# PSUM banks begun by ScalarE or VectorE with a summand, seven products for four more tiles, and three inverses on GpSimd, in a linear-attention block with a feed-forward part

## The chip, the cores and the metric

The kernel runs on one core of one Trainium2 chip. The metric is device time in microseconds of one execution; lower is better. The engines are named as in the profile: PE (TensorE products), PEld (its weight loads), DVE (VectorE), ACT (ScalarE), POOL (GpSimd) and SP (SyncE, which here only issues DMA). PSUM, where PE writes its products, has eight banks of 512 columns of 32 bits for each of the 128 partitions. All eight are one tile here, `banks`.

## What is computed

One transformer block over 2048 tokens of width 640, in bfloat16, with 32 heads of 20. First a linear attention with softmax features (Hedgehog), then a feed-forward part of width 1728, each behind a layer norm and with a residual:

```python
n   = layernorm(x)
q, k, v = n @ wqkv                        # 32 heads of 20
pq, pk  = q @ w_phi, k @ w_phi            # per head
phi_q = [softmax(pq), softmax(-pq)]       # 40 features; phi_k likewise
kv, z = phi_k^T v, sum over tokens of phi_k
o   = (phi_q @ kv) / (phi_q . z + 1e-6)
h   = x + o @ wo
out = h + silu(layernorm(h) @ w1) @ w2
```

## The kernel before

The tokens are cut into 16 tiles of 128. Everything of one tile is cut into named steps, such as `K3` (the keys of tile 3). The list `ORDER`, written out in full, gives the steps in the one order in which they are recorded; no scheduler moves them. Each step puts its instructions into the queues of its engines, and every queue runs in that order. So the order of steps decides what stands ahead of what on each engine, and semaphores between the engines do the rest.

The steps that the text names, with t the tile:

- `st`, `xn`: moments and normalised rows of x (L509, L528). `K`, `V`, `Q`: products with the key, value and query weights (L605, L643). `ex`, `su`, `rk`, `sc`: exponentials of the keys on ACT, their sums on DVE (L664), the inverses on ACT and the scaling on DVE (L677). `kv`: the sum over tokens phi_k^T v on PE (L696). `bd0`, `bd1`: DVE copies that sum out as a block-diagonal matrix after `kv15` (L705).
- `qe`: exponentials of the queries on ACT (L767). `qs`: their sums on DVE (L771). For tiles 0 to 5 `ql` takes the inverse as Ln and Exp on ACT (L782), `qi` the ratio of the two sums on POOL (L791) and `qr` the scaling on DVE (L802). For tiles 6 to 15 `qr` holds all three on DVE (L785, L791, L802). `qt`: a DMA transpose of the features.
- `D`: features times the block-diagonal matrix on PE (L851). `E`: inverse and division on DVE (L860, L861). `ot`: a DMA transpose. `G` with 0 or 1 for the half of the columns: products with wo on PE (L883), into a pair of banks. `ga`: DVE adds that pair to X, which from then on holds h (L890). `lm`, `ls`: sums and squares of h on ACT (L538, L543). `lr`: the inverse deviation on POOL in three small instructions, the middle one a power (L550, L553, L554). `hn`: the normalised rows on ACT (L560). `ht`: a DMA transpose.
- The feed-forward part goes by units: tiles 0 and 1, 2 to 5, 6 to 9, 10 to 13, 14 and 15. `u` and `s`: the plain way, products with w1 and the silu on ACT, one bank at a time (L966, L989); `u.L` (L977), `s.L` and `lt` are the last 64 columns. Units 6, 10 and 14 take another way for most of the columns: two by two blocks of weights and rows by seven products in place of eight (a Strassen form). It needs sums of weight blocks, `vw` (L1010, made once), and of row blocks, `vt` (L1020). Each group of two banks X and Y is filled by `vA` to `vE` on PE (L1047). Between them ACT saves intermediate states of bank Y into the tile `vr`: `vc1` both halves (L1059), `vc2` and `vc3` one (L1062). `va1` and `va0` add them to the banks on DVE (L1066), and `vs1`, `vs0` are the silus on ACT, from `vr` (L1072). So such a group is A, vc1, B, vc2, C, vc3, D, va1 in a chain between PE and ACT.
- The products with w2 take the seven-product form for every pair of tiles. `T` and `S` are sums of weights and of rows on DVE (L1120, L1137). `p1` to `p7` are the products on PE (L1155), 7 of 320 columns each. `p1`, `p5` and `p6` add up in bank a. `r1`, `r2`, `r3` and `r7` keep an intermediate state of a bank plus X in SBUF, on DVE (L1163). So `p6` waits for `r1`, which must have read bank a, and `p7` waits for `S3`. `w11`, `w12`, `w21` and `w22` add bank and kept state to the output tile on DVE (L1170). `out` stores it.

PSUM banks are handed out by `ps_half` and `ps_two` from a ring, the longest handed out first.

Of the kernel before, what the change touches and what calls it, by code (L numbers as in the profile page):

```python
# [36 lines left out]
qs9 lm2 u0.6 T1.2 s0.0 s0.L ga3 E4 qt6 u0.2 qr8 ls2 T2.2 qt7 s0.6 G50 u0.4 D6 lm3 T3.0 ls3 u0.12 qr9
T4.2 G51 s0.2 u0.10 E6 s0.4 s0.12 ot4 ga5 T3.2 T1.0 S3.0 lt0 u0.8 D7 E7 lr3 lr2 hn3 s0.10 hn2 qt8 G41
G40 p7.0 s0.8 T2.0 p2.0 D8 ot6 lm5 p1.0 ga4 T1.1 T4.0 S1.0 ht2 T2.1 ht3 ls5 lm4 padL1 S2.0 r1.0 G61 ls4
T4.1 r7.0 G60 S4.0 w11.0 p6.0 r2.0 ot7 lr5 E8 hn5 p4.0 lr4 w21.0 ga6 ht5 hn4 p5.0 ht4 p3.0 r3.0 G71 qs11  # L40
lm6 w22.0 qs10 ot8 qt9 G70 u2.L u2.10 w12.0 qr10 qt10 u2.5 ga7 u2.2 u2.9 qr11 u2.6 s2.5 s2.L s2.2 u2.11
s2.10 D9 qt11 s2.6 s2.9 qs12 out1 u2.0 qs13 lm7 out0 G81 E9 s2.11 qr12 D10 ot9 s2.0 G80 ga8 u2.4 D11
qt12 s2.4 ls7 E10 u2.1 u2.8 u2.3 qr13 ls6 qs15 G90 lm8 E11 G91 qs14 lr7 u2.12 ga9 ls8 s2.8 s2.3 lr8 lr6
# [33 lines left out]
def kernel(  # L77
# [65 lines left out]
    def ps_half():  # L143
        ring.append(ring.pop(0))
        return banks[:, ring[-1]]
# [1127 lines left out]
```

## Time and profile before

| | us |
|---|---|
| median of 2 runs (222.33 to 222.44) | 222.38 |
| the profiled execution, its own time | 222.19 |
| its span in the profile | 220.2 |
| PE busy | 215.3 |
| DVE busy | 196.5 |
| ACT busy | 166.1 |
| POOL busy | 71.8 |

The span runs from the first instruction to the end of the last; the execution's own time is about 2 us longer. The granted clock of TensorE is full throughout. A group's mean length of one instruction runs from its start to its end; the next one can start before that, so steps from start to start are shorter than the length. In the windows and in the chain, the first number is microseconds from the start of the span.

### The profile page before, as it was taken

To read this page: it belongs to the slowest core of one execution; us is meant where nothing else is said; L and a number is where in the kernel's file an instruction comes from. 1 tells how busy PE (TensorE), PEld (TensorE's weight loads), DVE (VectorE), ACT (ScalarE), POOL (GpSimd) and SP (SyncE) were. 2 spreads that over 40 slices of the span, in tenths; PEclk is the share of its full clock that TensorE was granted. 3 is DMA by queue.
4 is the path that set the end of the run, shared out by engine and by line. 5 is a ranking of instruction groups with operands and counts; after the bars stand their busy time and mean duration, and the time that the engine had idled before them with its cause. 6 is when DMAs were issued, how large, how long until landed. Compare 5 with 4: busy or idle time off the path is not lost.

```text
span 220.2 us, 5436 instructions
## 1 busy us (share of the span) xinstructions
PE 215.3 (98%) x2076; PEld 163.7 (74%) x2076; DVE 196.5 (89%) x352; ACT 166.1 (75%) x372; POOL 71.8 (33%) x136
## 2 busy tenths in 40 slices
PE   6999999999999999999999999999999999999994
PEld 4877777777777777887746577787888788887773
DVE  3999999999999999999999999999859955887984
ACT  6999899999879899997345986599879966474200
POOL 8399999979300140045000511340002200000000
PEclk9999999999999999999999999999999999999999
DMA  6999839947999786874586876553700124010202
GB/s 165 343 296 131 116 70 266 171 115 129 302 233 177 128 168 92 161 112 89 118 105 155 187 115 127 67 125 68 108 1 4 29 54 63 30 63 12 92 30 89
DMA packets 68159, 27.00 MB, mean 123 GB/s; under 512 B 61159, under 2 KB 67111, under 8 KB 68007
## 3 DMA queue, kind: packets, MB, share of 16 engines
q1 hardware_dynamic: 67335, 26.61, 58.7%
q8 instruction: 16, 0.26, 0.5%
q10 hardware_dynamic: 800, 0.06, 0.3%
q14 instruction: 8, 0.07, 0.1%
HBM read 9.55 MB, written 2.62 MB: 55 GB/s over the span
## 4 chain that ended last, share of the span: by engine, by line
PE 86%; DVE 10%; POOL 2%; issue 1%; ACT 0%; POOLq 0%
PE banks L1155 24%; PE banks L1047 13%; PE banks L605 11%; PE banks L966 11%; PE banks L883 10%; PE banks L643 9%; DVE st L509 4%; PE banks L851 3%; DVE Sk L664 2%; PE banks L696 2%; DVE xn L528 1%; PE banks L977 1%; DVE EK L677 1%; DVE mv L510 1%; DVE WTk L352 0%
## 5 line engine op out<-in xcount | busy, mean ns | idle before, releaser
L605 PEld LDWEIGHTS <-XnT 128*128 128x128 bf16 x300 | 28.4, 98 | 9.4
L528 POOL TENSOR_SCALAR xn<-X,mv,rs 128x640 bf16<-128x640 bf16 x12 | 31.5, 2626 | 0.6 <-ACT rs L518 0.4
L550 POOL TENSOR_SCALAR rs<-mv 128x1 f32<-128x1 f32 x16 | 3.8, 235 | 74.9 <-ACT xn L543 74.6
L1155 PEld LDWEIGHTS <-S 128*128 128x128 bf16 x224 | 21.5, 98 | 7.5
L1155 PE MATMUL banks<-T,S 128*128 128x320 bf16 x168 | 26.7, 299 | 0.0
L966 PE MATMUL banks<-HnT,w_sb 128*128 128x512 bf16 (+1 forms) x145 | 25.8, 328 | 0.0
L1066 DVE TENSOR_TENSOR vr<-banks,vr 128x512 f32<-128x512 f32 x30 | 20.0, 684 | 6.3 <-PE banks L1047 5.4
L883 PE MATMUL banks<-wo_sb,OT 128*128 128x320 bf16 x160 | 25.1, 299 | 0.0
L1072 ACT ACTIVATE shT<-vr 128x512 bf16<-128x512 f32 x30 | 18.1, 626 | 8.4 <-DVE vr L1066 8.3
L1047 PE MATMUL banks<-HnT,w_sb 128*128 128x256 bf16 (+1 forms) x144 | 24.3, 255 | 0.0
L643 PE MATMUL banks<-Wfq,XnT 128*128 128x342 bf16 (+2 forms) x160 | 22.7, 293 | 0.0
L605 PE MATMUL banks<-Wv,XnT 128*128 128x320 bf16 x150 | 22.3, 299 | 0.0
L664 DVE TENSOR_REDUCE Sk<-EK 128x64 f32<-128x1216 bf16 x16 | 21.9, 1391 | 0.2 <-ACT EK L660 0.2
L605 PE MATMUL banks<-Wfk,XnT 128*128 128x304 bf16 x150 | 21.6, 292 | 0.0
L660 ACT ACTIVATE EK<-banks 128x608 bf16<-128x608 f32 x32 | 20.2, 694 | 0.9 <-PE banks L605 0.5
L1155 PEld LDWEIGHTS <-shT 128*128 128x128 bf16 x175 | 16.6, 98 | 5.6
L966 PEld LDWEIGHTS <-w_sb 128*128 128x128 bf16 x145 | 13.8, 97 | 8.3
L883 PEld LDWEIGHTS <-OT 128*128 128x128 bf16 x160 | 15.4, 98 | 5.8
L1163 DVE TENSOR_TENSOR r<-banks,X 128x320 f32<-128x320 f32 x32 | 15.2, 483 | 5.0 <-PE banks L1155 4.9
L643 PEld LDWEIGHTS <-XnT 128*128 128x128 bf16 x160 | 15.0, 97 | 5.4
L989 ACT ACTIVATE shT<-banks 128x512 bf16<-128x512 f32 (+1 forms) x23 | 12.6, 571 | 7.0 <-PE banks L966 7.0
L1155 PE MATMUL banks<-w_sb,shT 128*128 128x320 bf16 (+2 forms) x119 | 17.7, 291 | 0.0
(121 smaller groups left out, 469.2 us busy)
## 6 DMA issues: line engine op xcount, KB each, us to landing
out_dram<-o_t SPq DMA_DIRECT2D x15, 160.0 KB, 1.9
w_sb<-in_B_w_dram SPq DMA_DIRECT2D x5, 432.0 KB, 5.2
w_sb<-in_B_w_dram SPq DMA_DIRECT2D x3, 480.0 KB, 5.2
X<-in_A_x_dram SPq DMA_DIRECT2D x1, 1280.0 KB, 8.5
Wk<-in_A_wqkv_dram SPq DMA_DIRECT2D x5, 160.0 KB, 3.4
Wv<-in_A_wqkv_dram SPq DMA_DIRECT2D x5, 160.0 KB, 6.2
wo_sb<-in_A_wo_dram SPq DMA_DIRECT2D x1, 800.0 KB, 5.0
X<-in_A_x_dram SPq DMA_DIRECT2D x1, 640.0 KB, 6.4
```

Of the source, the lines that this page charges most:

```text
L528: eng.tensor_scalar(out=xn_[t][:], in0=X[:, t, :], scalar1=mv_.pop(t)[:, 0:1], scalar2=rs_.pop(t)[:], op0=ALU.add if t in BY_ROWS else ALU ...
L605: nc.tensor.matmul(ps[:, g, 0:w], XnT[:, c, t * P : (t + 1) * P], W[:, c, g * w : (g + 1) * w], start=(c == 0), stop=(c == C - 1),)
L643: nc.tensor.matmul(ps[:, 0 : e - a], XnT[:, c, t * P : (t + 1) * P], Wfq[:, c, a:e], start=(c == 0), stop=(c == C - 1),)
L660: nc.scalar.activation(E5[:, :, :, b, 0:DR], p4, AF.Exp, scale=sign)
L664: nc.vector.tensor_reduce(sk[t][:], ek[t][:, 0 : H * HF].rearrange("p (q f) -> p q f", f=DH)[:, :, 0:DR], axis=AX.X, op=ALU.add)
L883: nc.tensor.matmul(ps_of["G", t][:, g, 0:HD], ot[t][:, c, :], wo_sb[:, c, g * HD : (g + 1) * HD], start=(c == 0), stop=(c == C - 1),)
L966: nc.tensor.matmul(ps[:, at : at + n], w1_sb[:, c, fc * P : fc * P + P], HnT[u][:, c, 0:n], start=(c == 0), stop=(c == C - 1),)
L1047: nc.tensor.matmul(vb_[u, i, bank][:, at : at + n], left[:, c, f * P : (f + 1) * P], right[:, c, :], start=bool(first) and q == 0 and c == ...
L1066: nc.vector.tensor_tensor(r, two(vb_.pop((u, i, "XY"[j]))), r, op=ALU.add)
L1072: nc.scalar.activation(rows_of(u)[:, f * n : (f + m) * n].rearrange("p (q b n) -> p b q n", q=m, b=2), vr_[u, i][:, 2 - 2 * j : 4 - 2 * j] ...
L1155: nc.tensor.matmul(ps[:, lo:hi], left[:, c, :], right[:, c, lo:hi], start=(c == 0 and k in FIRST), stop=(c == KS - 1 and k in LAST), skip_ ...
L1163: nc.vector.tensor_tensor(r_[t, name][:], ps_of[bank, t][:, 0:HD], X[:, t + i, g * HD : (g + 1) * HD], op=ALU.add)
```

## The change

Five things change together.

1. *Output projection.* `ga` now comes ahead of `G`: ACT copies X into the pair of banks, and the products of `G` add to it without starting the bank anew. `lm` reads h from the banks, writes it to X and takes its sum in the same ACT instruction. DVE has no part in it.
2. *Inner seven products.* `vc1` becomes two copies on ACT: one half of Y goes into bank X, the other to `vr`. `vc3` copies into the other half of X. `vE` adds its products to what stands in X, and `vs0` reads X directly. `va0` goes; `va1` stays. `vr` has two rows in place of four and three buffers in place of two.
3. *Unit of tiles 2 to 5* takes the seven-product form too (`BYSUMS`). So `vw` is wanted earlier, and there is a `vt` for that unit.
4. *Output products.* `r1` and `r3` write their sum (DVE) into the bank of `p2` and `p3`, which add to it. `w11` and `w12` become plain copies on ACT.
5. *Inverses of tiles 13 to 15* become a power on POOL with the ratio behind it on POOL; only the scaling stays on DVE.

A bank is now given back by `release`, after its last reader, and a seeded bank must have been covered by an earlier product. `ORDER` is written anew from the early steps on. The weight loads, the early phase's engines and the sizes of all other products are the same.

```diff
-    def ps_half():
-        ring.append(ring.pop(0))
-        return banks[:, ring[-1]]
+    def ps_half(key, cols=HD, seeded=0, readers=1):
+        k = next(k for k in ring if covered[k] >= seeded)
+        take(key, 0 if seeded else cols, [k], readers)
+        return banks[:, k]
...
     def row_mean(t):
         nc.scalar.activation(
-            xn_[t][:], X[:, t, :], AF.Identity, scale=-1.0 / (D * RD), accum_out=mv_[t][:, 0:1]
+            in_halves(t), ps_of.pop(("G", t))[:, :, 0:HD], AF.Identity, accum_out=mv_[t][:, 0:1]
         )
+        release(("G", t))
...
+    LATE_Q = 13
...
         if t < EARLY_Q:
             nc.scalar.activation(rm[:], ratios(t)[:, :, 1], AF.Ln)
             nc.scalar.activation(rm[:], rm[:], AF.Exp, scale=-1.0)
+        elif t < LATE_Q:
+            nc.vector.reciprocal(rm[:], ratios(t)[:, :, 1])
         else:
-            nc.vector.reciprocal(rm[:], ratios(t)[:, :, 1])
+            nc.gpsimd.tensor_tensor(rm[:], ratios(t)[:, :, 1], minus_t[:].to_broadcast([P, n]), op=ALU.pow)
...
-        eng = nc.gpsimd if t < EARLY_Q else nc.vector
+        eng = nc.vector if EARLY_Q <= t < LATE_Q else nc.gpsimd
...
     def residual(t):
-        xs = X[:, t].rearrange("p (g d) -> p g d", g=2)
-        nc.vector.tensor_tensor(xs, ps_of.pop(("G", t))[:, :, 0:HD], xs, op=ALU.add)
+        ps_of["G", t] = ps_two(("G", t), seeded=HD)
+        act(ps_of["G", t][:, :, 0:HD], in_halves(t))
     def out_projection(t, g):
...
-                start=(c == 0), stop=(c == C - 1),
+                start=False, stop=(c == C - 1), skip_group_check=True,
...
-    BYSUMS = (6, 10, 14)
+    BYSUMS = (2, 6, 10, 14)
...
     def inner_kept(u, i, which):
+        y = two(vb_[u, i, "Y"])
         if which == 1:
-            vr_[u, i] = pools["sums"].tile([P, 4, NU], F32, name="vr", bufs=2)
-            act(vr_[u, i][:, 1:3], two(vb_[u, i, "Y"]))
+            vb_[u, i, "X"] = ps_half((u, i, "X"), seeded=2 * NU)
+            vr_[u, i] = pools["sums"].tile([P, 2, NU], F32, name="vr", bufs=VRB)
+            act(two(vb_[u, i, "X"])[:, 0:1], y[:, 1:2])
+            act(vr_[u, i][:, 1:2], y[:, 0:1])
+        elif which == 2:
+            act(vr_[u, i][:, 0:1], y[:, 1:2])
         else:
-            k = {2: 0, 3: 3}[which]
-            act(vr_[u, i][:, k : k + 1], two(vb_[u, i, "Y"])[:, 1:2])
+            act(two(vb_[u, i, "X"])[:, 1:2], y[:, 1:2])
...
+    def seeded(t, bank, i, g, lo=0, hi=HD):
+        bank += "x" * (lo > 0)
+        ps_of[bank, t] = ps_half((bank, t), seeded=HD)
         nc.vector.tensor_tensor(
-            outs[t + i][:, g * HD + lo : g * HD + hi], ps_of[bank, t][:, lo:hi], r_[t, name][:, lo:hi], op=ALU.add
-        )
+            ps_of[bank, t][:, lo:hi], ps_of["a", t][:, lo:hi], X[:, t + i, g * HD + lo : g * HD + hi], op=ALU.add
+        )
+        release(("a", t))
...
+    def whole(t, bank, i, g, lo=0, hi=HD, eng="ACT"):
+        bank += "x" * (lo > 0)
+        copies[eng](out_of(t + i)[:, g * HD + lo : g * HD + hi], ps_of[bank, t][:, lo:hi])
+        release((bank, t))
```

Three stretches of the order, before and after, that the prediction speaks of. Early keys, before and after:

```
su3 K4 ref5 fq0 rs9 ex4 fq0e rs8 xt6 V4 wq2 ve4 su2 su4 V5 ve5 fq3 K5 rk2 xn7 ref6 xt7 rk3 xn8 fq3e sc2 K6 ex5 sc3 ex6 kv2
su3 K4 ref5 fq0 rs9 ex4 fq0e rs8 xt6 V4 wq2 ve4 V5 fq3 ref6 rk3 ve5 su2 rk2 xn7 xn8 wq4 K5 st15 xn9 K6 xt7 fq3e sc3 sc2 xt8 kv2
```

From the silu of unit 0 to `p6.0`, after:

```
G30 load9 qs11 ga5 s0.6 padL0 s0.L T1.2 s0.2 ls2 G31 G51 qt6 qt7 G50 T1.1 T2.0 T2.2 D6 qs10 ot4 lm5 u0.0 lm3 ls5 s0.10 lt0 qt8
u0.12 vw1.0 u0.4 T3.1 ga4 E6 s0.0 T2.1 T4.2 lr2 D7 s0.4 s0.12 u0.8 ot6 G41 G40 vw1.1 T3.2 qr11 s0.8 ls3 hn2 lm4 vw3.0 S3.0 S1.0
lr5 p1.0 S2.0 r1.0 p7.0 hn5 E7 p6.0 r7.0 ht2 lr3 D8 ls4 r2.0 p2.0 E8
```

From `qs13` to the late scalings, after:

```
qs13 ql13 qi13 vC.2.1 vD.2.0 va1.2.0 vc3.2.1 qt10 G71 ot8 vc1.2.2 vw3.1 vE.2.0 vA.2.3 vB.2.2 vs1.2.0 vs0.2.0 qr12 vD.2.1 G70
vw2.1 vc2.2.2 vC.2.2 vE.2.1 vc1.2.3 lm7 vc3.2.2 vs0.2.1 vB.2.3 vc2.2.3 va1.2.1 vs1.2.1 qs14 ql14 D9 vE.2.2 vC.2.3 vA.2.4 vD.2.2
vA.2.5 vw4.1 vs0.2.2 E9 vc3.2.3 vc1.2.4 ga8 vE.2.3 qt12 vB.2.4 va1.2.2 ot9 out1 vs0.2.3 vD.2.3 vc2.2.4 vs1.2.2 vc1.2.5 G81 vC.2.4
va1.2.3 G80 D10 vc3.2.4 lm8 vB.2.5 vD.2.4 vc2.2.5 out0 vE.2.4 ht6 ga9 qr13 qi14 qr14 vC.2.5 vc3.2.5 E10
```

More of the change, by code (lines that the diff above doesn't have):

```diff
@@ L39 @@
[L39 to L43, printed above, removed]
```

228 lines of the change are left out of this document (121 added, 107 removed).

## The prediction

> **What bounds the kernel now.** I read the page first, then the chain that ended last, then the engines' busy time in a stretch, then single instructions.
>
> ```profile
> span 220.2 us, 5436 instructions
> PE 215.3 (98%) x2076; PEld 163.7 (74%) x2076; DVE 196.5 (89%) x352; ACT 166.1 (75%) x372; POOL 71.8 (33%) x136
> PE 86%; DVE 10%; POOL 2%; issue 1%; ACT 0%; POOLq 0%
> ```
>
> The busy share of PE alone would not prove a bound, but the chain is 86% PE. Its pieces in order of time (start, length, line, count):
>
> ```profile
> 28.94 0.49 PE banks L696 x11
> ...
> 65.16 2.62 PE banks L643 x20
> ...
> 93.75 0.35 PE banks L851 x12
> ...
> 102.44 1.36 PE banks L883 x10
> 103.79 3.80 PE banks L1155 x28
> ...
> 109.54 6.47 PE banks L966 x30
> ...
> 158.27 3.49 PE banks L1047 x32
> ...
> 205.88 11.44 PE banks L1155 x91
> ```
>
> From 28.94 to 217.32 us one PE piece begins where the last ended. So there TensorE never waits, and the time falls only if it gets less work; any wait it meets is added in full. The next question is how much room the other engines have. This is busy time per stretch (columns: span, then PE, PEld, DVE, ACT, POOL with instruction counts, clock, DMA share, GB/s):
>
> ```profile
> 65.12:102.69 37.57, 37.57 (x390) 29.58 (x387) 36.80 (x63) 36.10 (x90) 8.02 (x21) 1.00 0.80 141
> 103.79:141.00 37.21, 37.21 (x310) 23.79 (x308) 36.09 (x65) 21.34 (x44) 7.99 (x20) 1.00 0.67 125
> ```
>
> From bd0 to r1.0 (65 to 103 us) PE, VectorE and ScalarE are all full. Afterwards ScalarE is at 57% and VectorE still at 97%. A change that shifts work from VectorE to ScalarE has room behind 104 us and hardly any ahead of it.
>
> **The change part by part.** *Products of tiles 2 to 5.* Twelve banks of five 512-column products go, six groups of eighteen 256-column products come. L966 runs 30 in 6.47 us, 216 ns each; L1047 runs 32 in 3.49 us, 109 ns each. 60 x 0.216 = 12.94 us against 108 x 0.109 = 11.78 us: **-1.16 us**, all on the path. No other product is added or removed.
>
> *The early order.* In VectorE's queue the second of two key scalings, sc2, releases kv2 on PE. Its neighbours:
>
> ```profile
> 19.77 0.87 DVE L509 BATCH_NORM_STATS2 st<-X 128x6 f32<-128x320 bf16 x2
> ...
> 20.80 1.29 DVE L528 TENSOR_SCALAR xn<-X,mv,rs 128x640 bf16<-128x640 bf16 x1
> ...
> 24.05 4.02 DVE L664 TENSOR_REDUCE Sk<-EK 128x64 f32<-128x1216 bf16 x3
> 27.98 1.55 DVE L677 TENSOR_TENSOR EK<-EK,Rk 128x1280 bf16<-128x1280 bf16 x2
> 29.45 0.88 DVE L509 BATCH_NORM_STATS2 st<-X 128x6 f32<-128x320 bf16 x2
> ```
>
> Before: su3, su2, su4 (1.31 us a step), then sc2 and sc3 (0.735 a step). After: su3, su2, st15 (19.77 to 20.80, 1.03), then sc3 and only then sc2. sc2 starts at 24.05 + 2.62 + 1.03 + 0.735 = 28.44 instead of 27.98, and PE, which does the same work ahead of kv2, waits **+0.45 us** longer.
>
> *VectorE ahead of p6.0.* r1.0 must have read bank a before p6.0 adds to it. The rows for the sums:
>
> ```profile
> 66.80 1.52 DVE L771 TENSOR_REDUCE Sq<-EQa 128x66 f32<-128x1320 bf16 x1
> 68.24 0.35 DVE L860 RECIPROCAL Rd<-banks 128x32 f32<-128x32 f32 x1
> ...
> 95.93 0.81 DVE L890 TENSOR_TENSOR X<-banks,X 128x640 bf16<-128x640 f32 x1
> 96.66 1.05 DVE L1120 TENSOR_TENSOR T<-w_sb 128x960 bf16<-128x960 bf16 x2
> ...
> 98.16 0.35 DVE L860 RECIPROCAL Rd<-banks 128x32 f32<-128x32 f32 x1
> 98.54 0.82 DVE L861 TENSOR_TENSOR O<-banks,Rd 128x640 bf16<-128x640 f32 x1
> 99.28 0.48 DVE L1120 TENSOR_TENSOR T<-w_sb,T 128x640 bf16<-128x640 bf16 x1
> ...
> 102.69 0.48 DVE L1163 TENSOR_TENSOR r<-banks,X 128x320 f32<-128x320 f32 x1
> ```
> ```profile
> L785 DVE RECIPROCAL Rq<-Sq 128x33 f32<-128x33 f32 x10 | 3.5, 354 | 0.0
> L791 DVE TENSOR_TENSOR Rho<-Sq,Rq 128x66 bf16<-128x66 f32 x10 | 2.3, 228 | 0.3
> L802 DVE TENSOR_TENSOR EQb<-EQb,Rho 128x660 bf16<-128x660 bf16 x7 | 3.5, 502 | 0.2
> L1010 DVE TENSOR_TENSOR SW<-w_sb 128x768 bf16<-128x768 bf16 x4 | 2.2, 547 | 0.0
> ```
>
> VectorE needs 37.57 us from bd0 (65.12) to r1.0 (102.69). Six additions ga leave this stretch (0.73 each, 95.93 to 96.66), E7 (98.16 to 99.28, 1.12) and T4.0 (0.48) move behind it: -6.0. But qs10 and qs11 (66.80 to 68.24, 1.44 each), qr11 (0.354 + 0.228 + 0.502 = 1.08) and vw1.0, vw1.1, vw3.0 (0.55 each) move ahead of it, the last three because SW sums are now wanted four tiles earlier: +5.6. Net -0.4, so r1.0 ends 37.2 + 0.48 = 37.7 us after bd0. On PE some blocks that stood ahead of p6.0 now stand behind it: D8 (0.35), G60 with G61 (1.36), p2.0 (a quarter of 3.80, 0.95), together 2.66. From 65.16 to 103.79 PE worked without a gap, 38.63 us; now 35.97. PE would come to p6.0 at 101.1 us and find r1.0 done at 102.8. It waits **+1.8 us**, with 0.1 for the semaphore (1.5 if the moved sums overlap their neighbours by 0.1 each, 2.2 if qr2, whose ql2 now stands behind qe3 on ScalarE, starts late). A wait on a seed ahead of p6.0 (ga2 before G21, ga3 before G30) lies inside this one, since VectorE's queue sets the later end.
>
> *Work moved to ScalarE.* Sixteen additions (L890) become seeds: a ScalarE copy of X into PSUM, ahead of G instead of behind. No ScalarE write into PSUM is in the trace. Rows near it:
>
> ```profile
> L538 ACT ACTIVATE xn<-X 128x640 bf16<-128x640 bf16 x16 | 11.9, 743 | 5.6 <-DVE X L890 4.7 <-DMA HnT<-xn 0.8
> L681 ACT CAST VP<-banks 128x640 bf16<-128x640 f32 x16 | 10.9, 685 | 0.1
> L989 ACT ACTIVATE shT<-banks 128x512 bf16<-128x512 f32 x21 | 12.0, 589 | 7.0 <-PE banks L966 7.0
> L1062 ACT COPY vr<-banks 128x256 f32<-128x256 f32 x30 | 10.8, 371 | 8.3 <-PE banks L1047 8.1
> L1072 ACT ACTIVATE shT<-vr 128x512 bf16<-128x512 f32 x30 | 18.1, 626 | 8.4 <-DVE vr L1066 8.3
> ```
>
> I bound a seed by 0.685 and 0.743 and take 0.72, the middle of the two. lm then reads PSUM instead of X, 0.06 less or the same. The Trainium skill ("ScalarE: Activation LUTs", section "Step-by-step: what each stage is for") holds that ScalarE reaches PSUM faster than SBUF; by it a seed would cost less than 0.685, and no run here shows it. From p6.0 to 141 us, eight seeds add 5.8 us, six groups of tiles 2 to 5 add 6 x (4 x 0.371 + 0.626 + 0.589) = 16.2 for the 12 x 0.589 = 7.1 that go, six last copies w11, w12 add 6 x 0.43 (between L1062 and L989): 21.3 + 5.8 + 9.1 + 2.6 = 38.8 us of durations for a stretch of 37.2 - 1.16 + 1.8 = 37.8. Of some 80 instructions each overlaps the next by about 0.1 us (VectorE's 0.81 long step took 0.73), so about 31 us: full, but possible. I cost it at nothing; the cover is the 16 us that ScalarE had free. VectorE loses fifteen additions va0 and the w11, w12 there; they lay beside PE work and gain nothing.
>
> *Late inverses.* Tiles 13 to 15 take the reciprocal as a power on GpSimd, with the product behind it:
>
> ```profile
> L553 POOL TENSOR_TENSOR rs<-rs,nhalf_t 128x1 f32<-128x1 f32 x16 | 10.9, 681 | 1.3
> L550 POOL TENSOR_SCALAR rs<-mv 128x1 f32<-128x1 f32 x16 | 3.8, 235 | 74.9 <-ACT xn L543 74.6
> L791 POOL TENSOR_TENSOR Rho<-Sq,Rq 128x66 bf16<-128x66 f32 x6 | 2.4, 394 | 17.1 <-ACT Rq L783 17.1
> ```
> ```profile
> OT<-O SPq DMA_TRANSPOSE x16, 2.6
> ```
>
> The last row, of the view of the transfers, is a transpose from issue to landing (2.6 us). A power over one column takes 0.68 us, 0.45 more than the plain L550; over 33 columns none is shown. It costs between 0.7 (columns free, as L791's 66 nearly are) and 0.24 + 33 x 0.45 = 15 us. I take 3 us, the middle in ratio. While it runs, qr14 waits on VectorE with E10 queued behind. E10 cannot begin before D10 has ended, and from qs13's place in the order to there PE has 63 of the 256-column products (6.9), four G halves (2.7) and two D (0.7): 10.3 us, of which qs13 takes 1.44 and 8.9 remain. Two powers and two products, one after the other, and qr14 must fit: 2X + 0.8 + 0.5 <= 8.9, X <= 3.8. Behind it E10 has a lead: G101 comes 6.2 us of products after D10, and E10 with its transpose needs 1.12 + 2.6, so about 2 us more of delay is free and X may be 4.8. At 3 us the cost is nothing.
>
> *Sum against the profiled execution* (222.19 us, 2 us around its span): -1.16 + 0.45 + 1.8 = +1.1, 223.3 us. The shown runs' median, 222.38, is 0.19 above it: **223.5 us**. Against 222.38 that is no change: 2% (4.4 us) is what a measurement of this kernel can tell.
>
> **The rivals.** *A. The products alone decide.* VectorE reaches r1.0 in time because its steps shrink or PE's early wait goes: 222.38 - 1.16 = 221.2, up to 222.4 with a part of the wait. For it: E7 and six ga did leave. Against: the count above has VectorE without a gap in that stretch.
>
> *B. Slower: the power blocks VectorE.* If one power costs X over 4.8 us, each microsecond more is paid twice, since qr14 waits for two. Over 2% slower, 226.8, wants 3.3 us more than the forecast, so it decides from X = 6.5, 0.2 us a column; at X = 8 the time is 230, at 10 it is 234. For it: the one-column row, if each column is paid anew. Against: L791, where 66 columns cost less than one power. The Trainium skill ("GPSIMD Engine Reference", section 3.1 "Elementwise — side-by-side cycle accounting") keeps elementwise work on VectorE, which speaks for B; its 2.6 cycles an element would make 33 columns nearly free, which speaks against it. No trace here settles it.
>
> *C. ScalarE becomes the bound* after p6.0: if its instructions overlap by 0.05 us instead of 0.1 and a tenth is lost to waiting in order (vc1 now stands between A and both B and E), 38.8 - 4 + 3.8 = 38.6 us stand against 37.8, and PE waits 1 to 3 us there: 224.6 to 226.8.
>
> **How the numbers follow.** Forecast (222.4 to 224.6) 0.55, A (221.0 to 222.4) 0.12, C 0.19, B 0.14. The range 221.5 to 227.0 leaves out a part of A and nearly all of B. Faster by over 2% would need 4.4 us from a change that removes 1.16 us of PE work: 0.01, out of A; slower 0.14, from B; the rest is within 2%.
>
> **What would show it.** L1047's successor with 324 + 108 products, PE busy about 1.2 us less in work; kv2 at about 29.4; a PE gap of 1 to 2 us ahead of the first p7.0 and p6.0 with VectorE's S or r as releaser; VectorE without gaps before it. B shows as POOL rows of over 5 us and VectorE waiting on POOL near 125 us; C as PE waits on ScalarE copies between 104 and 140 us. The forecast is wrong if PE shows no gap near 101 us, or gaps behind it that add up to over a microsecond.

## The result, and the profile after

The changed kernel takes 244.52 us (median of 243.48 and 245.57) against 222.38 us: 1.100 times as long, 95% interval 1.079 to 1.120. The forecast was 223.5 us, the range 221.5 to 227.0. So the change is 22 us slower, 10 times what the forecast's own bad terms came to.

First the page of the kernel after: span, busy time, the chain by engine, and the busy tenths of PE with the granted clock, in 40 slices of 6.1 us.

```profile
span 243.5 us, 5588 instructions
PE 221.8 (91%) x2124; PEld 170.8 (70%) x2124; DVE 175.6 (72%) x309; ACT 187.2 (77%) x444; POOL 89.1 (37%) x143
...
PE   7899999999999979579996697299999999999995
...
PEclk9999999999999999959999999779999999999999
...
PE 45%; POOL 15%; DVE 15%; ACT 8%; issue 8%; DMA 6%; SPq 1%; DVEq 0%; ACTq 0%; POOLq 0%
```

Before, PE was busy for 98% of the span and 86% of the chain. Now it is 45% of the chain, and GpSimd, which was 2%, is 15%. The row of PE shows three holes: slices 17 and 18 (97 to 110 us), 22 and 23 (128 to 140) and 25 and 26 (146 to 158). Behind the first and the last the clock row falls too. What PE waited for, from the view of the waits (line, releaser, total, times, longest):

```profile
PE banks L904 <- ACT banks L900: 6.9, 3, 5.7
PE banks L877 <- DVE O L887: 5.9, 2, 3.9
PE banks L1051 <- DVE SW L1014: 1.4, 1, 1.4
PE banks L968 <- DMA HnT<-xn: 1.1, 1, 1.1
```

L900 is the seed `ga`, L877 is `D`, L1014 is `vw`, L968 is `u`. Before, PE had no such wait behind 29 us.

The rest of this document needs a ledger. For each product of the trace I take the time from its start to the next start, less the median of that for its size. The sum of the medians is PE's work: 212.93 us before and 211.79 after, so **-1.14 us**. What is over the median is time lost:

| us lost by PE | 0 to 20 | 20 to 66 | 66 to 95 | 95 to 112 | 112 to 125 | 125 to 145 | 145 to 165 | all |
|---|---|---|---|---|---|---|---|---|
| before | 3.2 | 0.3 | 0 | 0 | 0 | 0 | 0 | 3.3 |
| after | 4.2 | 1.2 | 2.6 | 6.8 | 0.1 | 4.6 | 8.3 | 27.7 |

(For the kernel after the third and fourth columns part at 100 us.) -1.1 of work and +24.4 lost make the 23.3 us between the two spans. Behind 165 us nothing is lost. Three places hold 19.7 of the 24.4.

**The first hole, 100 us.** VectorE's instructions in order of time (start, length, and in brackets the idle time before with its releaser):

```profile
96.27 1.52 DVE L795 TENSOR_REDUCE Sq<-EQb 128x66 f32<-128x1320 bf16 x1
102.63 0.56 DVE L1014 TENSOR_TENSOR SW<-w_sb 128x768 bf16<-128x768 bf16 x1 [4.84 <-DMA EqT<-EQa]
...
103.89 0.82 DVE L887 TENSOR_TENSOR O<-banks,Rd 128x640 bf16<-128x640 f32 x1
```

The 0.56 us sum is `vw1.0`. It waits 4.84 us for a DMA transpose that it has no data from. The tile SW, which it writes, lies in memory that held EQa, the early query features, and the last step that reads EQa is the transpose `qt8`. The queue of the DMAs shows why that is late:

```profile
96.50 1.20 SPq L896 DMA_TRANSPOSE OT<-O  x1
97.81 1.18 SPq L1110 DMA_TRANSPOSE shT<-SHL  x1
99.03 1.47 SPq L839 DMA_TRANSPOSE EqT<-EQa  x1
```

SyncE issues in order, and `qt8` stands behind `ot4` and `lt0`. In this trace the queue stood at `ot4` until 96.50 us, by the view of the waits for products of `G` on PE; the silu that `lt0` needs had ended at 96.3 us. The transpose issued at 99.03 us lands at 102.6, and `vw1.0` starts. E6 stands behind `vw1.0` on VectorE, and D7 on PE behind E6:

```profile
98.02 2.89 PE L968 MATMUL banks<-HnT,w_sb 128*128 128x256 bf16 x25
104.77 0.74 PE L877 MATMUL banks<-KVB,EqT 128*128 128x63 bf16 x12 [3.85 <-DVE O L887]
105.33 2.30 PE L968 MATMUL banks<-HnT,w_sb 128*128 128x256 bf16 x10
```

Ten products of 256 columns took 2.30 us. In the row above, 25 of them took 2.89, so ten would be 1.16. By the ledger PE lost 2.9 us more behind the wait, with work at hand. The clock column of the windows (the third number from the end, 0.50 in the two rows) says why, for this hole and for the last one:

```profile
103.70:110.50 6.80, 5.73 (x34) 3.75 (x34) 6.15 (x13) 2.32 (x5) 1.16 (x3) 0.50 0.33 28
...
154.90:161.70 6.80, 5.09 (x20) 2.83 (x20) 2.81 (x6) 4.10 (x8) 1.90 (x4) 0.50 0.27 51
```

The Trainium skill ("TensorE: Matmul & The Clock Gate", section "Part 1: The HAM clock gate (the "warmup" mystery)") says that the array falls to half rate after an idle window of about 3.4 us, and comes back after about as long at work. The two waits here, 3.9 and 5.7 us, agree with the first half; the slow work behind them lasted longer, 5.7 and 5.1 us (PE's busy time in the two rows).

**The other two holes.** The groups of the page that matter, with busy time and mean ns of one:

```profile
L811 POOL TENSOR_TENSOR Rq<-Sq,minus_t 128x33 f32<-128x33 f32 x3 | 17.6, 5859 | 5.2 <-DVE Sq L795 5.2
...
L582 ACT ACTIVATE xn<-X,rs 128x640 bf16<-128x640 bf16 x16 | 14.6, 924 | 6.4 <-POOL rs L576 6.4
```

One power over 33 columns takes 5.86 us. GpSimd in order of time:

```profile
123.84 5.67 POOL L811 TENSOR_TENSOR Rq<-Sq,minus_t 128x33 f32<-128x33 f32 x1 [3.28 <-DVE Sq L795]
129.60 0.32 POOL L817 TENSOR_TENSOR Rho<-Sq,Rq 128x66 bf16<-128x66 f32 x1
131.56 5.92 POOL L811 TENSOR_TENSOR Rq<-Sq,minus_t 128x33 f32<-128x33 f32 x1 [1.64 <-DVE Sq L795]
137.55 0.31 POOL L817 TENSOR_TENSOR Rho<-Sq,Rq 128x66 bf16<-128x66 f32 x1
...
147.06 5.98 POOL L811 TENSOR_TENSOR Rq<-Sq,minus_t 128x33 f32<-128x33 f32 x1 [0.24 <-DVE Sq L795]
153.12 0.31 POOL L817 TENSOR_TENSOR Rho<-Sq,Rq 128x66 bf16<-128x66 f32 x1
153.52 0.50 POOL L572 TENSOR_SCALAR rs<-mv 128x1 f32<-128x1 f32 x1
```

Two things on VectorE wait for the first two:

```profile
129.95 1.53 DVE L795 TENSOR_REDUCE Sq<-EQb 128x66 f32<-128x1320 bf16 x1 [2.99 <-POOL Rho L817]
...
137.90 0.50 DVE L828 TENSOR_TENSOR EQb<-EQb,Rho 128x660 bf16<-128x660 bf16 x1 [3.23 <-POOL Rho L817]
```

The second is `qr14`, which the prediction had. The first is not a reader of the result: it is `qs14`, which writes new sums into the buffer that the ratio `qi13` has yet to read. The third power holds up something else again, on ScalarE:

```profile
155.04 0.92 ACT L582 ACTIVATE xn<-X,rs 128x640 bf16<-128x640 bf16 x1 [6.39 <-POOL rs L576]
155.87 1.30 ACT L900 CAST banks<-X 128x640 f32<-128x640 bf16 x2
```

The row at 153.52 on GpSimd is `lr7`, behind the third power; `hn7` on ScalarE waits for it; `ga11`, the seed of tile 11, stands behind `hn7`; and PE waits 5.66 us for the seed and then runs twenty products in 5.38 us (twice 1.36 before).

### The profile page after: what moved, and what is told of

Read it like the earlier page. It is cut to its first block, busy times and chain, and to the rows that moved or that the text cites. A ratio compares the mean times of both kernels' runs of the same rounds, so it can differ in the third digit from the quotient of the medians.

```text
span 243.5 us, 5588 instructions
## 1 busy us (share of the span) xinstructions
PE 221.8 (91%) x2124; PEld 170.8 (70%) x2124; DVE 175.6 (72%) x309; ACT 187.2 (77%) x444; POOL 89.1 (37%) x143
## 4 chain that ended last, share of the span: by engine, by line
PE 45%; POOL 15%; DVE 15%; ACT 8%; issue 8%; DMA 6%; SPq 1%; DVEq 0%; ACTq 0%; POOLq 0%
PE banks L1168 18%; PE banks L1051 12%; POOL Rq L811 7%; PE banks L904 6%; POOL xn L548 5%; DVE Sq L795 5%; PE banks L627 4%; DVE O L887 3%; DMA Wv<-in_A_wqkv_dram 2%; ACT EQb L789 2%; PE banks L968 2%; DMA OT<-O 2%; DMA EqT<-EQa 1%; DVE Rd L886 1%; ACT EK L682 1%
## 5 line engine op out<-in xcount | busy, mean ns | idle before, releaser
L904 PE MATMUL banks<-wo_sb,OT 128*128 128x320 bf16 x160 | 28.5, 330 | 7.2 <-ACT banks L900 6.9
L1051 PE MATMUL banks<-HnT,w_sb 128*128 128x256 bf16 (+1 forms) x192 | 32.4, 259 | 0.0
L572 POOL TENSOR_SCALAR rs<-mv 128x1 f32<-128x1 f32 x16 | 4.7, 294 | 68.4 <-ACT xn L565 68.1
L904 PEld LDWEIGHTS <-OT 128*128 128x128 bf16 x160 | 16.7, 106 | 15.5 <-issue 7.5
L1168 PEld LDWEIGHTS <-S 128*128 128x128 bf16 x224 | 21.5, 98 | 7.7
L1074 DVE TENSOR_TENSOR vr<-banks,vr 128x512 f32<-128x512 f32 x21 | 14.3, 685 | 15.5 <-PE banks L1051 13.3
L1051 PEld LDWEIGHTS <-w_sb 128*128 128x128 bf16 x240 | 21.5, 98 | 3.4
L1051 PE MATMUL banks<-ST,SW 128*128 128x256 bf16 (+1 forms) x144 | 23.2, 259 | 0.0
L627 PE MATMUL banks<-Wfk,XnT 128*128 128x304 bf16 x150 | 21.5, 292 | 0.3 <-ACT VP L703 0.3
L1051 PEld LDWEIGHTS <-SW 128*128 128x128 bf16 x192 | 17.2, 98 | 4.2 <-DVE SW L1014 1.7
L582 ACT ACTIVATE xn<-X,rs 128x640 bf16<-128x640 bf16 x16 | 14.6, 924 | 6.4 <-POOL rs L576 6.4
L811 POOL TENSOR_TENSOR Rq<-Sq,minus_t 128x33 f32<-128x33 f32 x3 | 17.6, 5859 | 5.2 <-DVE Sq L795 5.2
```

The lines of the kernel that those rows point to most:

```text
L582: nc.scalar.activation(xn_[t][:], X[:, t, :], AF.Identity, scale=r[:, 0:1], bias=r[:, 1:2])
L627: nc.tensor.matmul(ps[:, g, 0:w], XnT[:, c, t * P : (t + 1) * P], W[:, c, g * w : (g + 1) * w], start=(c == 0), stop=(c == C - 1),)
L811: nc.gpsimd.tensor_tensor(rm[:], ratios(t)[:, :, 1], minus_t[:].to_broadcast([P, n]), op=ALU.pow)
L904: nc.tensor.matmul(ps_of["G", t][:, g, 0:HD], ot[t][:, c, :], wo_sb[:, c, g * HD : (g + 1) * HD], start=False, stop=(c == C - 1), skip_gro ...
L1051: nc.tensor.matmul(vb_[u, i, bank][:, at : at + n], left[:, c, f * P : (f + 1) * P], right[:, c, :], start=bool(first) and q == 0 and c == ...
L1074: nc.vector.tensor_tensor(r[:], two(vb_.pop((u, i, "Y"))), r[:], op=ALU.add)
```

## The experiments

First theory P: the three powers make the holes behind 125 us. First rival S: the early VectorE order makes the loss and the rest follows from it. Second rival C: ScalarE has too much work.

**A multiplication in the power's place.** Same operands, shape, place and waits; only the price of the instruction differs. The output then lacks the inverses of tiles 13 to 15.

```diff
-            nc.gpsimd.tensor_tensor(rm[:], ratios(t)[:, :, 1], minus_t[:].to_broadcast([P, n]), op=ALU.pow)
+            nc.gpsimd.tensor_tensor(rm[:], ratios(t)[:, :, 1], minus_t[:].to_broadcast([P, n]), op=ALU.mult)
```

> Kernel after, with the power on GpSimd replaced by a multiplication of the same two operands and the same 128x33 shape (three times). The output then lacks the inverse of the query sums of tiles 13 to 15; every instruction, wait and place in the queues is otherwise that of after. Theory P (the power's own length, 5.7 to 6.0 us each, holds up VectorE through qs14 and qr14 and ScalarE through lr7, hn7 and the seed of G11): the multiplication takes about 0.4 us, the PE waits near 130 to 138 us (1.6 + 0.9 + 2.2) and 150.6 us (5.8, with 2.4 more of slow products behind it) go, 12 to 13 us in all: about 232 us. Rival S (VectorE's sums vw1.0 at 100 us and the early order make the loss): the time falls by under 3 us, 242 or more. Rival C (ScalarE has too much work since the seeds): the wait at 150.6 us stays with ScalarE as releaser, 238 to 242 us.

Measured: 233.51 us (232.59 to 234.42), 1.049 of before (1.038 to 1.059). The multiplication takes 0.42 us, a fourteenth of the power:

```profile
L811 POOL TENSOR_TENSOR Rq<-Sq,minus_t 128x33 f32<-128x33 f32 x3 | 1.3, 422 | 7.4 <-DVE Sq L795 7.4
```

PE's loss between 125 and 165 us goes from 12.9 to 0.2 us, the one near 100 us stays (6.8). P holds for the later holes. The early loss stands by itself, and C has no wait over 0.2 us left behind 112 us.

**`qt8` early.** Ahead of `qt6`, so that SyncE issues it before `ot4` and `lt0`.

```diff
-G31 G51 qt6 qt7 G50 T1.1 T2.0 T2.2 D6 qs10 ot4 lm5 u0.0 lm3 ls5 s0.10 lt0 qt8
+G31 G51 qt8 qt6 qt7 G50 T1.1 T2.0 T2.2 D6 qs10 ot4 lm5 u0.0 lm3 ls5 s0.10 lt0
```

> Kernel after, with the one step qt8 (the last DMA transpose that reads the tile EQa of the early query features) moved ahead of qt6, so that SyncE issues it before the transposes that wait for ScalarE's silu of unit 0. Theory S: the tile SW of vw1.0 lies where EQa lay, so vw1.0 waits for that transpose; with it early, VectorE's wait of 4.8 us ahead of vw1.0 and PE's of 4.0 us at 100.6 us go, with the slow products behind it (2.4 us): 5 to 6.5 us, about 239 us. Theory P alone: nothing here, since the later waits take up whatever comes earlier: 244 us. Rival V (VectorE's queue ahead of p6.0 is over full, as the prediction has it): the wait at 100.6 us goes, but 1.5 to 2 us of it come back ahead of p6.0: 240.5 us.

Measured: two executions, 240.33 and 244.16 us, too far apart for a ratio; the kernel after had 243.48 and 245.57. The trace, of the longer one, is clear where the times are not: VectorE's wait at `vw1.0` falls from 4.84 to 2.15 us, and PE's loss near 100 us from 6.8 to 2.5 us. But between 125 and 145 us it rises from 4.6 to 6.3. PE now comes earlier to the powers and waits longer there, and 0.3 us more behind: nearly half of the 4.3 us is given back.

**Both.**

```diff
-            nc.gpsimd.tensor_tensor(rm[:], ratios(t)[:, :, 1], minus_t[:].to_broadcast([P, n]), op=ALU.pow)
+            nc.gpsimd.tensor_tensor(rm[:], ratios(t)[:, :, 1], minus_t[:].to_broadcast([P, n]), op=ALU.mult)
...
-G31 G51 qt6 qt7 ... s0.10 lt0 qt8
+G31 G51 qt8 qt6 qt7 ... s0.10 lt0
```

> Both edits: multiplication in place of the power (the inverses of tiles 13 to 15 are left out of the output) and qt8 ahead of qt6. If the two causes are separate, the gains add: 12.5 + 5.5, about 226 us, and the 3 to 4 us above the kernel before are early waits and ga seeds. With the prediction's wait ahead of p6.0 (1.8 us) back in the trace: 227 to 228 us. Rival C (ScalarE overloaded): PE waits with ScalarE as releaser between 104 and 140 us, 229 us or more.

Measured: 228.89 us (227.74 to 230.03), 1.028 of before (1.015 to 1.040). Against the multiplication alone `qt8` is worth 4.6 us by the medians (2.6 to 6.7 by the single executions) and by the ledger (6.8 to 2.2 us near 100 us), when no power takes it back. What is left of PE's waits behind the first 10 us is small and spread, and no single one is over 1 us:

```profile
PE banks L904 <- ACT banks L900: 0.8, 2, 0.6
PE banks L968 <- DMA HnT<-xn: 0.6, 1, 0.6
PE banks L627 <- DMA XnT<-xn: 0.6, 1, 0.6
PE banks L877 <- DVE O L887: 0.6, 1, 0.6
PE banks L1168 <- DVE banks L1185: 0.5, 1, 0.5
```

In the ledger: 1.5 us between 20 and 66 us, 2.2 from 66 to 95, 2.2 from 95 to 112, 0.5 behind. The expected 226 us was 3 too low, and the 227 to 228 us with the prediction's wait ahead of p6.0, which is nearer to what the trace shows, 1 to 2.

**The power alone, in the kernel before.** Only the fifth part of the change.

```diff
-            nc.vector.reciprocal(rm[:], ratios(t)[:, :, 1])
+            nc.gpsimd.tensor_tensor(rm[:], ratios(t)[:, :, 1], minus_t[:].to_broadcast([P, n]), op=ALU.pow)   # t >= 13
```

> Kernel before, with only the fifth part of the change: the inverses of tiles 13 to 15 as a power on GpSimd with the ratio behind it, in the places of the order where VectorE had them. Theory P as a property of the power: three instructions of 5.7 to 6.0 us each again. What they cost here depends on who stands behind them; with VectorE's scalings and GpSimd's inverse deviations behind them as in after, 8 to 13 us: 230 to 235 us. If the cost needs the seeds of the output projection (a chain from GpSimd through ScalarE to PE that before doesn't have), it is clearly less: 224 to 229 us. The prediction's own rule (each microsecond over 4.8 paid twice) gives 222.4 + 2 x (5.8 - 4.8) = 224.4 us.

Measured: 238.93 us (238.08 to 239.78), 1.073 of before (1.063 to 1.082). That is 16 us for three small instructions, more than I expected, and without any seed. GpSimd, ScalarE and PE in order of time:

```profile
126.21 5.67 POOL L790 TENSOR_TENSOR Rq<-Sq,minus_t 128x33 f32<-128x33 f32 x1 [2.12 <-DVE Sq L774]
131.96 0.31 POOL L796 TENSOR_TENSOR Rho<-Sq,Rq 128x66 bf16<-128x66 f32 x1
132.23 5.66 POOL L790 TENSOR_TENSOR Rq<-Sq,minus_t 128x33 f32<-128x33 f32 x1
137.97 0.31 POOL L796 TENSOR_TENSOR Rho<-Sq,Rq 128x66 bf16<-128x66 f32 x1
138.25 0.23 POOL L553 TENSOR_SCALAR rs<-mv 128x1 f32<-128x1 f32 x1
```
```profile
140.84 0.92 ACT L563 ACTIVATE xn<-X,rs 128x640 bf16<-128x640 bf16 x1 [15.16 <-POOL rs L557]
```
```profile
142.96 2.05 PE L1160 MATMUL banks<-T,S 128*128 128x320 bf16 x7 [12.77 <-DVE S L1142]
```

Two powers stand back to back, and `lr` behind both. ScalarE's `hn` waits 15.2 us, a silu stands behind it, a sum S on VectorE waits for the silu, and PE for S: 12.8 us, and then a half clock. So the queue that matters is GpSimd's own. It holds every tile's layer norm, and through `hn` all of ScalarE.

**`lr7` ahead of the third power** (with `qt8` early).

```diff
-ls7 S1.2 G100 D13 qt14 qs15 ql15 qi15 p7.2 ... ht8 lr7 p5.2 hn7
+ls7 lr7 S1.2 G100 D13 qt14 qs15 ql15 qi15 p7.2 ... ht8 p5.2 hn7
```

> Kernel after with qt8 early (as in the run of qt8 alone, 242.25 us), and the one step lr7 (GpSimd's inverse deviation of tile 7, three small instructions) moved ahead of the third power, right behind ls7. The powers stay. Theory Q (the third power costs by what is queued behind it on GpSimd: lr7, on which hn7 and behind that the seed of G11 wait on ScalarE): PE's wait of 5.7 us near 150 us goes, and the 2.6 us by which the twenty products behind it are slow: about 234 us. Rival, the prediction's own queue (only VectorE's scalings wait for the powers): the third power cost nothing there, so nothing changes, 242 us. Half way, if VectorE's qr15 and the seeds behind it become late in its place: 237 to 239 us.

Measured: 235.21 us (234.63 to 235.79), 1.057 of before (1.053 to 1.062). Three instructions moved past one give back 7 us by the medians (5 to 9 by the two executions without this edit), and no power has become shorter (5.75 us on average). In the ledger the loss from 145 to 165 us falls from 8.6 to 1.7 us. The wait of 5.7 us and the slow products behind it are gone. In their place PE waits 1.6 us where `qr15`, now the first to need that power, holds up VectorE:

```profile
PE banks L1168 <- DVE o_t L1196: 1.6, 1, 1.6
```

**A third buffer for Sq** on top of that.

```diff
-        sq[t] = pools["att"].tile([P, NCH, 2 * HC], F32, name="Sq")
+        sq[t] = pools["att"].tile([P, NCH, 2 * HC], F32, name="Sq", bufs=3)
```

> The kernel of the run with lr7 ahead of the third power and qt8 early (235.21 us), and three buffers for the sums Sq in place of two. The powers stay. Theory: qs14 on VectorE writes into the buffer of Sq that the ratio qi13 on GpSimd, behind the first power, must have read; that is why VectorE waits 3.0 us near 126 us, and PE 1.4 us for the weight sum vw4.1 and 0.7 us for the seed of G81. With a third buffer these go, and the second power still starts when the first ends, so VectorE's wait for qr14 (3.2 us) stays and grows or shrinks little: 233 us. Rival: qs14's wait is only traded for qr14's, since two powers of 5.7 us stand ahead of qr14 in any case; then VectorE waits over 5 us there and PE as much as before: 235 to 236 us.

Measured: 233.89 us (233.49 to 233.98), 1.050 of before (1.043 to 1.057). VectorE no longer waits at `qs14`, and PE not for `vw4.1` and the seed of G81. The wait for `qr14` stays, and now D11 gets all of it (VectorE, then PE):

```profile
132.26 0.50 DVE L828 TENSOR_TENSOR EQb<-EQb,Rho 128x660 bf16<-128x660 bf16 x1 [3.32 <-POOL Rho L817]
```
```profile
133.95 0.52 PE L877 MATMUL banks<-KVB,EqT 128*128 128x63 bf16 x12 [2.75 <-DVE O L887]
```

So the buffer was a cause of the middle hole, but only 1.3 us of the time hung on it; PE's loss from 125 to 145 us hardly moved (4.7 and 4.5), since the two powers ahead of `qr14` remain. What fell is the loss from 145 to 165 us, from 1.7 to 0.5: PE's wait behind `qr15` went from 1.6 to 0.2 us.

**A power over 11 columns** (with `qt8` early, the other columns multiplied).

```diff
+            for lo, hi, op in ((0, 11, ALU.pow), (11, n, ALU.mult)):
```

> Kernel after with qt8 early, and each power over 11 of the 33 columns; the other 22 columns get a multiplication (so two thirds of the inverses of tiles 13 to 15 are left out of the output). It measures the power's price by columns and the prediction's rule that a power of up to 4.8 us is free. If the price goes by columns (0.55 us for one, 5.9 for 33, so 0.17 each): 2.2 us for 11 columns, 2.6 us with the multiplication. By the prediction's rule that is free: as with the multiplication alone, 228 to 229 us. If the price is one of the instruction and not of its columns: 5.5 us or more, 240 to 242 us. If it goes by columns but the slack is smaller than the prediction said: 230 to 235 us.

Measured: 231.40 us (231.30 to 231.49), 1.040 of before (1.038 to 1.043). The groups by shape, and PE's first wait:

```profile
L812 POOL TENSOR_TENSOR Rq<-Sq,minus_t 128x11 f32<-128x11 f32 x3 | 6.9, 2309 | 5.0 <-DVE Sq L795 4.9
L812 POOL TENSOR_TENSOR Rq<-Sq,minus_t 128x22 f32<-128x22 f32 x3 | 0.9, 310 | 0.0
```
```profile
PE banks L907 <- ACT banks L903: 2.9, 3, 2.0
```

One column takes 0.55 us, 11 take 2.31 and 33 take 5.67 to 5.98: about 0.16 us a column and 0.4 once. The price goes by columns. But 2.6 us, well under the 4.8 that the prediction called free, still cost 2.5 us more than the multiplication: `ga11` is late again, and the products behind it are slow. The slack behind the third power is smaller than the one the prediction looked at.

**Without the late inverses**, `qt8` early.

```diff
-    LATE_Q = 13
+    LATE_Q = 16
```

> Kernel after with qt8 early and without the fifth part: the inverses and ratios of tiles 13 to 15 are back on VectorE, as in the kernel before; nothing is left out. VectorE gets 3 x (0.35 + 0.23) = 1.7 us back between 125 and 150 us, where it is busy 20.1 of 25 us in the run with the multiplication and qt8 early (228.9 us). If that room holds it: 228 to 229 us, 2.5% over the kernel before, all of it now waits ahead of 107 us. If VectorE becomes the bound there: 229 to 231 us.

Measured: 228.27 us (228.20 to 230.70), 1.030 of before (1.022 to 1.038). That is as fast as with the multiplication (228.89), so VectorE had the room. The profile of this run is of its longest execution, 230.70 us; where the ledger of a later run is compared with it, it is that one.

**VectorE's work ahead of p6.0 made shorter.** Weight sums and three steps of the queries go behind; `qs12`, `qs13` and `qt11` move a little further back with them.

```diff
-... D6 qs10 ... vw1.0 ... vw1.1 T3.2 qr11 s0.8 ls3 hn2 lm4 vw3.0 S3.0 S1.0 lr5 p1.0 S2.0 r1.0
+... r1.0 p7.0 hn5 E7 p6.0 r7.0 vw1.0 vw1.1 vw3.0 ... w22.0 qs11 qr11 qt11 ... hn6 qs10 qr10
```

> The kernel of the run before this one, and VectorE's work ahead of p6.0 made shorter: qs10, qs11 and qr11 (1.44 + 1.44 + 1.08 us) go behind w22.0 (qs12 and qs13 a little further too), and the weight sums vw1.0, vw1.1, vw3.0 (0.5 us each, and what vw1.0 waits for) behind r7.0. The prediction's step says that VectorE's queue ahead of r1.0 is what PE waits for near p6.0, 2.2 us in all between 95 and 107 us. If so, these waits go: 226 to 227 us. If other waits set PE there (seeds on ScalarE, the transposes of h), they stay and the time too, 228 to 229 us. If the moved sums are late behind p6.0 (VectorE is full until 118 us), PE waits there in its place: 228 to 230 us.

Measured: 232.77 us (231.45 to 233.23), 1.045 of before (1.040 to 1.051): slower than without this edit. The loss from 95 to 112 us falls from 2.5 to 1.4 us as the step says, but from 112 to 145 it rises from 1.0 to 4.9. The first group of tiles 2 to 5 waits for its weight sums:

```profile
PE banks L1050 <- DVE SW L1013: 2.1, 2, 1.9
```

**Only the weight sums behind r7.0.**

```diff
-... lt0 u0.12 vw1.0 u0.4 ... G40 vw1.1 T3.2 qr11 s0.8 ls3 hn2 lm4 vw3.0 S3.0 ... p6.0 r7.0 ht2
+... lt0 u0.12 u0.4 ... G40 T3.2 qr11 s0.8 ls3 hn2 lm4 S3.0 ... p6.0 r7.0 vw1.0 vw1.1 vw3.0 ht2
```

> Kernel after without the powers and with qt8 early, and only the weight sums vw1.0, vw1.1 and vw3.0 moved from ahead of r1.0 to behind r7.0; qs10, qs11 and qr11 stay (unlike in the run that moved both and came out at 232.77 us). VectorE loses 1.5 us of work and a wait of 1.6 us ahead of r1.0. By the prediction's step (VectorE sets r1.0, PE waits for it, 2.2 us in all near p6.0) PE gains up to 2 us there; VectorE has 1.5 us more to do before vA.2.0 and the vE of the first group, and it is full until 125 us. If that is late: it is paid again at the first products of tiles 2 to 5, 228 us in all. If it is not: 226.3 us.

Measured: 228.30 us (228.16 to 228.88), 1.026 of before (1.024 to 1.029). The same 1.4 us from 95 to 112 us, and 0.3 more behind. The medians, with 228.27 for the kernel without this edit, show no gain. One profile each can't say where the 0.8 us went that the ledger has left; it stays open.

**The early order of the kernel before**, ahead of `bd0` (one stretch of it):

```diff
-V5 fq3 ref6 rk3 ve5 su2 rk2 xn7 xn8 wq4 K5 st15 xn9 K6 xt7 fq3e sc3 sc2 xt8 kv2
+su2 su4 V5 ve5 fq3 K5 rk2 xn7 ref6 xt7 rk3 xn8 fq3e sc2 K6 ex5 sc3 ex6 kv2
```

> Kernel after without the powers and with qt8 early (228.27 us), and the steps ahead of bd0 in the order of the kernel before. The prediction costed the new early order at 0.45 us more, by sc2 behind st15 and sc3. If that is all, and it is undone: 227.8 us, and PE waits ahead of 66 us come down from about 1.8 us to the 0.45 us of the kernel before. If the new early order saves something later that the old one does not (qe3, ql2 and Q7 stand ahead of bd0 there and stay ahead of it here): no change or slower, 228.3 to 229.

Measured: 227.34 us (226.69 to 229.75), 1.024 of before (1.015 to 1.033). PE's loss from 20 to 66 us falls from 1.7 to 0.6 us. 0.4 us of it comes back between 66 and 95 us, with a new wait of 0.7 us of a D for the transpose of its features. By its median it is the fastest variant, 0.9 us below the kernel without this edit, which is within the spread of the two. It is slower than the kernel before, and so are all others.

**Two tiles without seeds.** ADDED holds the tiles 0 and 1; VectorE adds behind G as before.

```diff
     def residual(t):
+        if t in ADDED:
+            nc.vector.tensor_tensor(in_halves(t), ps_of.pop(("G", t))[:, :, 0:HD], in_halves(t), op=ALU.add)
```

> Kernel after without the powers and with qt8 early, and the output projection of tiles 0 and 1 in the way of the kernel before: G begins its banks, and VectorE adds them to X behind it; ScalarE makes no seed for these two. Nothing is left out. In the run without the powers ScalarE is busy without a gap from 73 to 95 us, and PE waits there 0.5 us (OT), 0.7 (seed of G21) and 1.1 (rows of tiles 0 and 1). Theory C (ScalarE is full there since the seeds, so that work moved to it was not free as the prediction had it): ScalarE gets back 1.3 us, PE's waits near 86 and 90 us go down by 1 to 1.5 us in all; but VectorE gets 1.5 us more ahead of r1.0, and the wait near p6.0 grows by as much or less: 227.5 to 228.5 us. If ScalarE is not what is late there: waits near 86 and 90 us as they were and VectorE's work on top, 229.5 to 230 us.

Measured: 231.75 us (231.30 to 232.61), 1.042 of before (1.038 to 1.046): slower, against both expectations. The window of the run that it starts from has DVE 21.4 and ACT 21.5 busy of 22 us:

```profile
73.00:95.00 22.00, 19.68 (x189) 14.98 (x187) 21.42 (x35) 21.49 (x61) 3.16 (x10) 1.00 0.83 121
```

Taking the two seeds away did free ScalarE (it now waits for VectorE), and PE's waits for the seed of G21 and for the rows of tiles 0 and 1 went. PE waits at another place, for a bank that E3 on VectorE has still to read, with a half clock behind it:

```profile
79.95 0.74 ACT L561 ACTIVATE xn<-X 128x640 bf16<-128x640 bf16 x1 [1.96 <-DVE X L906]
```
```profile
86.37 4.40 PE L671 MATMUL banks<-Wfq,XnT 128*128 128x342 bf16 x20 [2.46 <-DVE O L893]
```

By these rows neither engine has room there. The loss from 66 to 95 us goes from 2.8 to 5.4 us. The banks are handed out differently too, so these 2.6 us are not VectorE's alone.

## Why the prediction was wrong

*Products of tiles 2 to 5* (-1.16): right, -1.14 us.

*The early order* (+0.45): the sign is right, the size low. The loss from 20 to 66 us is 0.9 us more in the kernel after and mostly 0.9 to 1.4 more in the other runs. With the old order it is 0.3 more. The wait that the step names, of kv2 for sc2, is 0.5 to 0.8 us in six of these runs; 0.29 before and the forecast's 0.45 make 0.74; in the kernel after it does not show, and PE waits 0.46 us for transposed rows near 26 us in its place. The step followed VectorE alone; there are also waits for such rows, and of 0.26 us for a ScalarE copy near 58 us.

*VectorE ahead of p6.0* (+1.8): about right in size, partly by luck, and hidden in the kernel after by the larger hole. With `qt8` early the loss from 95 to 112 us is 2.1 to 2.5 us, with VectorE at work all but without a gap, other than 1.6 to 2.2 us at `vw1.0`. p6.0 itself has only 0.6 of it; D7 and the product that waits for S have 1.1, also behind VectorE, and the rest, D6, waits for a transpose. What the step left out cost more: it counted `vw1.0` by its 0.55 us and did not ask what its tile waits for. Memory that is handed over is a wait like any other, and SyncE's queue ends it. That is missing in the prediction: about 4.5 us, counted as nothing.

*Work moved to ScalarE* (nothing): the price of a seed was right: 0.722 us on average against 0.72 taken. The Trainium skill's rule that ScalarE reaches PSUM faster ("ScalarE: Activation LUTs", section "Step-by-step: what each stage is for") would have made it less than 0.685; the trace does not show that. The cover was wrong. The 16 us of free ScalarE lay behind 104 us, as the prediction itself read from its two windows; but six seeds stand ahead of it, where ScalarE had 1.5 us free. PE loses 2.1 to 3.2 us between 66 and 95 us, where it lost nothing, in all runs that keep the seeds: its waits there are for a seed, for a transpose of O and for the rows of tiles 0 and 1. Rival C fits that, in another stretch than it named: behind 112 us no ScalarE wait over 0.2 us is left once the powers are gone, but for two in the run that moved VectorE's steps. That ScalarE's work is the cause is argued and not shown, since two seeds fewer made the kernel slower.

*Late inverses* (nothing): this step failed, and most of the error is here: 11 us by the multiplication in the full change, 16 us alone in the kernel before. Two parts of it were wrong. The price, 3 us as the middle in ratio between 0.7 and 15, was 5.86; the row over one column was the nearest and spoke for a price by column. But with the right price the prediction's rule, twice what is over 4.8 us, still gives only 2 us. The larger fault was the queue. The prediction followed the reader of the result (`qr14`, E10) and did not list what else stands behind the instruction on GpSimd (`lr7`, then `hn7` and `ga11` on ScalarE) nor who wants the buffer that it reads (`qs14`). Moving `lr7` alone was worth 7 us. The prediction's own signs for this came: gaps behind 101 us that add up to over a microsecond (13 us of loss behind 112 us), POOL rows of over 5 us, and VectorE waiting on POOL. Rival B, given 0.14, had the side and the engine, but it used the same rule, and its 6.5 us for a slowdown of 2% was too mild: 5.86 us cost 11, and 2.6 us already 2.5.

*The sum.* It added waits as if PE ran at full clock behind them. The two long holes cost 2.9 and 2.6 us more, in slow products.

What is settled: 11 to 13 us are the powers, about 4.5 us `qt8` and `vw1.0`, and about 6 us what is left without both (1.030 of before): the early order, the full ScalarE and VectorE from 66 to 95 us, and VectorE ahead of p6.0, less the 1.1 us of saved products. How these last parts share it is shown only within about 1 us, since each edit moved a wait elsewhere.

## What to carry to other kernels

When a step moves to an engine that seems idle, list everything that stands behind it in that engine's queue and follow each to the bound engine; here a nearly idle engine with short, urgent instructions had the least room for a long one. Ask of every moved step which buffer it writes and who must have read it. And here, with the bound engine at 98%, two engines beside it were full as well for a stretch: room is to be read for the stretch where the work lands, not for the whole span.

## What the runs showed of the hardware

- A power on GpSimd costs by columns: 0.55, 2.31 and 5.67 to 5.98 us for 1, 11 and 33, where a multiplication over 33 takes 0.42 and VectorE's reciprocal 0.35. The Trainium skill ("GPSIMD Engine Reference", section 3.1 "Elementwise — side-by-side cycle accounting") keeps elementwise work on VectorE, and these runs agree; its figure of 2.6 cycles an element doesn't hold for a power.
- In these runs the clock falls to half behind waits that are shorter than the 3.4 us of the Trainium skill ("TensorE: Matmul & The Clock Gate", section "Part 1: The HAM clock gate (the "warmup" mystery)"). The first row is the window behind a wait of 2.0 us in the run with 11 columns, the second the one behind another wait of 2.0 us, in the kernel after. The third lies behind a wait of 1.4 us and across one of 0.7, in the run with `lr7` moved; the same two waits in the kernel after left the clock full (the clock is the third number from the end):

```profile
143.30:147.50 4.20, 4.14 (x19) 2.48 (x19) 2.78 (x6) 2.61 (x7) 1.78 (x3) 0.59 0.36 68
```
```profile
139.50:143.00 3.50, 3.42 (x46) 2.80 (x46) 2.76 (x6) 1.68 (x4) 0.49 (x2) 1.00 0.50 98
```
```profile
129.10:132.50 3.40, 3.08 (x13) 1.75 (x13) 1.14 (x3) 2.52 (x7) 3.40 (x1) 0.50 0.64 163
```

  Behind a wait of 2.5 us (two tiles without seeds) and one of 2.75 us (third buffer) the clock was at half for 3.4 us as well, and behind the two long waits of the kernel after for 6.8 us each. So waits of 1.4 to 2 us may cost only themselves, or nearly 2 us more in slow products.
